# One-bank PSUM items for the S5 half of a kernel that runs a state-space layer beside a long convolution

## The chip, the cores and the metric

The kernel runs on one core of one Trainium2 chip. The metric is the device time of one execution in microseconds (us). The core has four engines that matter here: TensorE (PE, matrix products into PSUM; its weight loads are listed as PEld), VectorE (DVE), ScalarE (ACT) and GpSimd (POOL). SyncE (SP) issues nearly all transfers (DMA). Each engine takes its instructions in the order in which they were written, and waits where an instruction needs a result of another engine.

PSUM holds eight banks; a bank takes 512 fp32 values on each of 128 partitions. In this kernel it is four tiles of two banks each.

## The reference

Two independent parts are computed from their own inputs and laid side by side in the output (2048 positions, 640 columns each, bf16).

```python
# A: a diagonal complex state-space layer (S5), 640 states
dt = exp(log_dt);  Lam_bar = exp(dt * Lam)
B_bar = ((Lam_bar - 1) / Lam)[:, None] * Bmat
Bu = einsum("bld,pd->blp", x, B_bar)
for t in range(L):                      # L = 2048
    h = Lam_bar * h + Bu[:, t, :]
y = 2 * einsum("blp,dp->bld", hseq, Cmat).real + x * Dskip

# B: H3, a 4-tap shift, a gate, a convolution as long as the sequence, a gate
kv = shift(k, shift_k) * v
y = irfft(rfft(pad(kv)) * rfft(pad(ssm_k)))[:S] + kv * ssm_D
return q * y
```

## The kernel before, in words

**Part A.** The 2048 positions are dealt into eight classes c (position modulo 8) of M = 256 positions; the 640 states into five blocks j of 128. In the tile `u{j}` each class has a real and an imaginary plane (r = 0, 1) of 256 columns. For every j the kernel forms, on TensorE, the input products of classes 1 and 5 together (item `u1{j}`), 3 and 7 together (`u3{j}`), 2 and 6 together (`v{j}`), class 4 (`w{j}`) and class 0 (`z{j}`). All of them are products of the transposed weights `BT` with the transposed input `xT` (L460 for pairs of classes, L468 for a single class), five matmuls over the input columns for each plane. `v`, `w` and `z` also gather earlier classes: the function `join` (L475, L476) adds matmuls whose weights are diagonal matrices of powers of the decay (`diagL{j}`, written by item `dL{j}`) and whose data are classes already evicted to `u{j}`. Each product is evicted from PSUM to `u{j}` by an item with an e behind its letter (`ue`, `ve`, `we`, `ze`), by a copy on ScalarE (L144) or VectorE (L146). Then VectorE runs the scan over class 0 (`rs{j}`, `ro{j}`), and the other classes are restored from it: `m{c}{j}` scales by the decay into the tile `tmp` (three instructions, L312 on ScalarE or L314 on VectorE) and `r{c}{j}` adds twice on VectorE (L522).

The outputs are 16 blocks of 128 positions by 640 columns. Item `p{n}` computes one on TensorE: for each half of 320 columns ten matmuls of `u` with `Cs` (L534), and for the first three blocks some small ones for the term x * Dskip (L541). For the other 13 blocks that term is read from the input again (`xl{n}`, a transfer; `xm{n}`, a product at L563), and VectorE adds it while it evicts the block (`ye{n}`, L549). The first three are evicted by ScalarE. `yd{n}` stores a block. Blocks 0 and 1 need class 0 of all j, 2 and 3 class 4, 4 to 7 the classes 2 and 6, 8 to 11 the classes 1 and 5, 12 to 15 the classes 3 and 7. The output staging tile `yo` holds four blocks, and so does the staging of `xl`.

**Part B.** The 640 channels go through in five groups G of 128. A group's stages: `kT`, `vT` (transposing loads), `tap` (the shift, TensorE) and `kv` (VectorE, L625), `kvo` and `kvs` (to memory and back in another order), `hs` (the filter), `s1h`, `s1k` (first transform stage, TensorE L639) with their evictions to the tile As (`s1he`, `s1ke`), `s2` (second stage, L657) with evictions to the tile XH (`s2e`), the spectral product `y` in two halves (VectorE, L671 to L674), `inv` (inverse, L685) with evictions `zs` to the tile zz, `zt` (two transposing transfers of zz), `fin` (last stage, L707), `ob` (product with q on VectorE, L712, for which `qi` loads q) and `od` (store). Each transform item fills a two-bank tile and is evicted by one instruction of 1024 values a partition. `ks` are copies of kT into kS for the shift.

**Order.** A plan (`make_plan`) lists the items with engine, dependences and costs. The order in which they are issued is a written list, `ORDER`, one word for an item. `u10@6` means that item `u1` of block 0 uses the PSUM tile 6 // 2 = 3; a `v` behind it (`ue12@2v`) puts an eviction or a scaling on VectorE, otherwise it runs on ScalarE; `a` and `b` are the two halves of `tmp`. At the end of the kernel a loop walks the list and calls each item's function with its tile. All engines and the queue of SP follow this one list, each with its own items.

The names of the two staging values that the order depends on are `NPS = 4` (PSUM tiles) and `NYO = 4`, `NXR = 4` (output and input staging).

Of the kernel before, what the change touches and what calls it, by code (L numbers as in the profile page):

```python
# [9 lines left out]
ALU = mybir.AluOpType  # L10
# [10 lines left out]
NT = 5  # L21
T = 8
M = L // T
# [4 lines left out]
NYO = 4  # L28
NSK = 13
NXR = 4  # L30
NTAB = 3
# [16 lines left out]
class Kernel:  # L48
# [406 lines left out]
    def pe_u(self, j, c, joins, ps):  # L455
        mm = self.nc.tensor.matmul
        x = self.__dict__[f"xT{c}"]
        for r in range(2):
            for k in range(NT):
                mm(ps[:, r, :], lhsT=self.BT[:, r, k, j * 128:(j + 1) * 128], rhs=x[:, :, k, :],  # L460
                   start=(k == 0), stop=(not joins and k == NT - 1))
        self.join(j, joins, ps, lambda c2, r: self.pair(j, c2, r), 2 * M)

    def pe_w(self, j, c, joins, ps):
        mm = self.nc.tensor.matmul
        for r in range(2):
            for k in range(NT):
                mm(ps[:, r, 0:M], lhsT=self.BT[:, r, k, j * 128:(j + 1) * 128], rhs=self.xc(c)[:, k, :], start=(k == 0), stop=False)  # L468
        self.join(j, joins, ps, lambda c2, r: self.u(j, c2, int(c2 > c))[:, r, :], M)

    def join(self, j, joins, ps, src, n):
        mm = self.nc.tensor.matmul
        for r in range(2):
            for i, (s, c2) in enumerate(joins):
                mm(ps[:, r, 0:n], lhsT=self.dl(j)[:, 3 * s, :], rhs=src(c2, r), start=False, stop=False)  # L475
                mm(ps[:, r, 0:n], lhsT=self.dl(j)[:, 3 * s + 2 - r, :], rhs=src(c2, 1 - r), start=False, stop=(i == len(joins) - 1))  # L476

    def ev_u(self, eng, j, c, ps):
        out = self.__dict__[f"u{j}"][:, c::4, :, 2:2 + M].rearrange("p c r m -> p r c m")
        self.copy(eng, out, ps[:].rearrange("p r (c m) -> p r c m", c=2))  # L480

    def ev_half(self, eng, j, c, ps):
        self.copy(eng, self.u(j, c), ps[:, :, 0:M])
# [20 lines left out]
    def classes(self, j, c):  # L504
        u = self.__dict__[f"u{j}"]
        if c == 4:
            return 1, 6, u[:, 0:1, :, 2:2 + M], u[:, 4:5, :, 2:2 + M]
        if c == 2:
            return 2, 3, u[:, 0::4, :, 2:2 + M], u[:, 2::4, :, 2:2 + M]
        return 2, 0, u[:, c - 1::4, :, 2:2 + M], u[:, c::4, :, 2:2 + M]  # L510
# [13 lines left out]
    def pe_proj(self, c, i, skip, ps):  # L524
        mm = self.nc.tensor.matmul
        ts = slice(128 * i, 128 * i + 128)
        xT = self.xc(c)
        for b in range(2):
            o = ps[:, b, :]
            c0 = 320 * b  # L530
            for j in range(NT):
                h = self.u(j, c)
                for r in range(2):
                    mm(o[:, 0:320], lhsT=h[:, r, ts], rhs=self.Cs[:, r, j, c0:c0 + 320], start=(j == 0 and r == 0),  # L534
                       stop=(skip and j == NT - 1 and r == 1))
            if skip:
                continue
            pieces = [(d, max(c0, d * 128), min(c0 + 320, d * 128 + 128)) for d in range(NT)]
            pieces = [q for q in pieces if q[1] < q[2]]
            for q, (d, lo, hi) in enumerate(pieces):  # L540
                mm(o[:, lo - c0:hi - c0], lhsT=xT[:, d, ts], rhs=self.diagD[:, d, lo - d * 128:hi - d * 128],  # L541
                   start=False, stop=(q == len(pieces) - 1))

    def ev_y(self, eng, n, ps):
        out = self.yo[:, n % NYO, :].rearrange("q (b n) -> q b n", b=2)
        self.copy(eng, out, ps[:, :, 0:320])

    def dve_yx(self, n, ps):
        self.nc.vector.tensor_tensor(out=self.yo[:, n % NYO, :].rearrange("q (b n) -> q b n", b=2), in0=ps[:, :, 0:320],  # L549
                                     in1=self.xr(n).rearrange("q (b n) -> q b n", b=2), op=ALU.add)  # L550
# [168 lines left out]
def make_plan(K):  # L719
# [96 lines left out]
    for c in (1, 5, 3, 7, 2, 6, 4, 0):  # L816
        dmat(f"x{c}", 1.4, 0.3275, (), lambda c=c: K.load_x(c))
    for j in range(NT):
        bt = [f"bte{j}_{x}" for x in range(2)] if j < JB else [f"B{(j - 1) // 2 * 2 + 1}"]
        A(f"dL{j}", "AD", 2.6, ["lam", "dc"] + ([f"z{j - NDL}"] if j >= NDL else []), lambda eng, j=j: K.diagL(eng, j), lat=0.12, dve=1.25)  # L820
        for c in (1, 3):
            pe(f"u{c}{j}", 10 * P512, 20, [f"x{c}", f"x{c + 4}"] + bt + [f"wm{w}" for w in range(WARM)], lambda ps, j=j, c=c: K.pe_u(j, c, (), ps), f"u{c}{j}")
            ev(f"ue{c}{j}", 1024, [f"u{c}{j}", "zer"], lambda eng, ps, j=j, c=c: K.ev_u(eng, j, c, ps), f"u{c}{j}")
        pe(f"v{j}", 14 * P512, 28, ["x2", "x6", f"dL{j}", f"ue1{j}"] + bt, lambda ps, j=j: K.pe_u(j, 2, ((0, 1),), ps), f"v{j}")
        ev(f"ve{j}", 1024, [f"v{j}", "zer"], lambda eng, ps, j=j: K.ev_u(eng, j, 2, ps), f"v{j}")
        pe(f"w{j}", 18 * P256, 36, ["x4", f"dL{j}", f"ue3{j}", f"ve{j}"] + bt, lambda ps, j=j: K.pe_w(j, 4, ((0, 3), (1, 2)), ps), f"w{j}")
        ev(f"we{j}", 512, [f"w{j}", "zer"], lambda eng, ps, j=j: K.ev_half(eng, j, 4, ps), f"w{j}")
        pe(f"z{j}", 22 * P256, 44, ["x0", f"we{j}"] + bt, lambda ps, j=j: K.pe_w(j, 0, ((0, 7), (1, 6), (2, 4)), ps), f"z{j}")
        ev(f"ze{j}", 512, [f"z{j}"], lambda eng, ps, j=j: K.ev_half(eng, j, 0, ps), f"z{j}")
        dve(f"rs{j}", 2.2, [f"ze{j}", f"tab{j}", "lam"], lambda j=j: K.dve_scan(j))  # L830
        dve(f"ro{j}", 1.08, [f"rs{j}"], lambda j=j: K.dve_out(j))
        for c in (4, 2, 1, 3):
            src, raw = {4: ("ro", "we"), 2: ("r4", "ve"), 1: ("r4", "ue1"), 3: ("r2", "ue3")}[c]
            A(f"m{c}{j}", "AD", 1.36 if c == 4 else 2.23, [f"{src}{j}"], lambda eng, buf, j=j, c=c: K.re_mul(eng, j, c, buf), lat=0.12,
              dve=0.73 if c == 4 else 0.9, take=f"R{c}{j}")
            dve(f"r{c}{j}", 0.75 if c == 4 else 1.28, [f"m{c}{j}", f"{raw}{j}", f"z{j}"], lambda buf, j=j, c=c: K.dve_re(j, c, buf), give=f"R{c}{j}")
    zs_all = [f"{x}{j}" for j in range(NT) for x in ("u1", "u3", "v", "w", "z")]
# [3 lines left out]
    for n, (c, i) in enumerate(seq):  # L841
        hs = [f"r{'o4'[c // 4] if c % 4 == 0 else c % 4}{j}" for j in range(NT)]
        skip = n >= 16 - NSK
        pe(f"p{n}", 20 * P320 + 0.3 * (not skip), 40 + 14 * (not skip), hs + cs_all + ["dD"], lambda ps, c=c, i=i, skip=skip: K.pe_proj(c, i, skip, ps), f"p{n}")
        free = f"yd{n - NYO}" if n >= NYO else f"cs{NT - 1}"
        if skip:
            dma(f"xl{n}", "SP", 0.43, 0.107, [f"ye{n - NXR}"] if n >= 16 - NSK + NXR else zs_all, lambda c=c, i=i, n=n: K.load_xr(c, i, n))
            dve(f"xm{n}", 0.4, [f"xl{n}", "dbc"], lambda n=n: K.dve_xm(n))
            dve(f"ye{n}", 0.78, [f"p{n}", f"xm{n}", free], lambda ps, n=n: K.dve_yx(n, ps), give=f"p{n}")
        else:  # L850
            ev(f"ye{n}", 640, [f"p{n}", free], lambda eng, ps, n=n: K.ev_y(eng, n, ps), f"p{n}")
        dma(f"yd{n}", "SP", 0.43, 0.107, [f"ye{n}"], lambda c=c, i=i, n=n: K.store_y(c, i, n))
# [48 lines left out]
zer pc x5 pc2 lv dc B0 wt wm1@0 x1 wm2@2 gp3 dc2 pv@4 exp@4 vec@4 pp2 pc3 zd pp B1 x7 hk rho Fi wm3@6 bt0_1@0 rr bt0_0@2 l_sk aM  # L901
x3 bte0_0@2 bte0_1@0v x6 x2 trig1 lam gam dL0@v dL1@v kT0 G3 hp1 wm0@4 dD u10@6 nG3 u11@0 dcol ue10@6 x4 u12@2 u30@4 ue12@2v hp0
tp0 sk gp1 ks0_1@v vT0 gp2 gp0 G2 ue11@0 v0@6 x0 ue30@4 i64 dS0 tab0 hs0 u31@0 ve0@6 ks0_0@v aR dco dM w0@4 ue31@0v tp2 nG2
tap0_1@2 dR tap0_0@6 B3 we0@4v z0@0 tp1 kv0_1@2 tab1 tp3 kv0_0@6 G1 had0 s1h0_3@4 G0 dS1 H1 dL2@v s1h0_2@2 s1h0_0@6 ze0@0 rs0
ro0 m40@av tab2 v1@0 s1he0_3@4 u13@4 H0 r40@a nI kvo0 kT1 tp4 ve1@0 ks1_0@v tab3 vT1 s1he0_2@2 w1@0 ks1_1@v m20@bv tap1_0@2
r20@b kv1_0@2 nG0 s1he0_0@6 tap1_1@6 kv1_1@6 ue13@4 we1@0 m10@a r10@a s1h0_1@4 s1he0_1@4 z1@0 ze1@0 kvs0 s1k0_3@2 s1k0_2@6 dL3@v
s1ke0_2@6 hs1 s1ke0_3@2 rs1 ro1 u34@4 ue34@4 s1k0_0@0 nG1 s1ke0_0@0 s1k0_1@6 s1ke0_1@6 tab4 v3@2 ve3@2 dS2 had1 s20_2@4 s2e0_2@4
s20_0@0 m30@bv s2e0_0@0v s20_1@6 s2e0_1@6 s20_3@2 s2e0_3@2v kT2 s20_4@4 s20_5@0 s20_6@6 kvo1 s2e0_4@4 s2e0_5@0 m41@av s20_7@2
s2e0_7@2 ks2_1@v s2e0_6@6v u14@4 ue14@4 s1h1_2@0 s1h1_1@2 s1he1_2@0 r41@a s1he1_1@2 CT1 kvs1 vT2 u33@6 s1h1_0@4 ue33@6 s1k1_0@0
ks2_0@v CT0 tap2_0@2 y0_0 tap2_1@6 s1ke1_0@0 s1he1_0@4 s1k1_3@0 s1ke1_3@0 kv2_0@2 kv2_1@6 kT3 s1h1_3@2 y0_1 inv0_0@4 zs0_0@4  # L910
s1k1_1@0 inv0_1@6 zs0_1@6 ca0 s1ke1_1@0v cs0 s1he1_3@2 v2@4 kvo2 ve2@4 inv0_2@6 zs0_2@6 inv0_3@2 s1k1_2@0 dS3 w3@4 s1ke1_2@0
s21_5@6 hs2 ks3_0@v m11@av zs0_3@2 ks3_1@v had2 s21_6@0 we3@4 r11@a s21_4@2 s2e1_4@2v ca1 s2e1_6@0 vT3 zt0_1 u32@4 s2e1_5@6
ue32@4 s21_7@0 s2e1_7@0 kvs2 cs1 ca2 s21_3@2 tap3_0@6 kv3_0@6 tap3_1@4 s2e1_3@2 w2@0 we2@0 s21_2@6 s21_0@2 kv3_1@4 s2e1_2@6
# [22 lines left out]
def kernel(  # L936
# [26 lines left out]
    with tc.manual_schedule():  # L963
        for n, _, how in names:
# [7 lines left out]
            elif tiles:  # L972
                args.append(tiles[0])
# [31 lines left out]
```

## Time and profile before

| | |
|---|---|
| timed runs, median of 3 | 197.34 us (195.78 to 197.46) |
| profiled execution | 197.87 us, its span 195.8 us |
| TensorE busy | 179.1 us, 3135 matmuls |
| VectorE busy | 176.1 us, 365 instructions |
| ScalarE busy | 150.7 us, 199 instructions |
| mean granted TensorE clock | 0.983 |
| 16 DMA engines, the transfers' queue | 89.6% of the span |

A row of the groups reads: line, engine, operation, output and inputs by the program's names, partitions and elements, count; then busy us and the mean ns of one; then idle time of the engine just before, and what ended it. A row of the stretches reads: from and to, length, then busy us of PE, PEld, DVE, ACT and POOL with instruction counts, the granted TensorE clock, the DMA share and GB/s. A row in order of time reads: start, duration, engine, line, operation, count.

### The profile page before, as it was taken

The page shows a single profiled execution, that of the slowest core. Times are in us where ns is not written, and L with a number is a line of the kernel's source. Part 1 is how long each engine was busy: PE and PEld are TensorE (multiplying, and loading weights), DVE is VectorE, ACT ScalarE, POOL GpSimd, SP SyncE. Part 2 cuts the span into 40 slices and gives each one's busy share as a digit, 9 for nine tenths or more (in the row PEclk, how much of TensorE's full clock was granted, in tenths as well). Part 3 has the DMA queues.
Part 4 walks back from the last instruction along what each step waited for, and adds up shares of the span by engine and source line. Part 5 has one row for each costly group of instructions (what it writes and reads, how often), then busy time and mean ns, then how long its engine had stood idle before and what let it go on. Part 6 is the DMA issues. An engine that isn't in the chain of part 4 may idle for free. (4 is left out here: it accounts for less than half of the span.)

```text
span 195.8 us, 7219 instructions
## 1 busy us (share of the span) xinstructions
PE 179.1 (91%) x3135; PEld 123.1 (63%) x3135; DVE 176.1 (90%) x365; ACT 150.7 (77%) x199; POOL 19.7 (10%) x46
## 2 busy tenths in 40 slices
PE   7399999999989999999999866999989999999992
PEld 2144456467474557688667655777677778777771
DVE  1579999999999989999999999999999999998672
ACT  2488478998898999989989899998999794840000
POOL 8874060300000000000000000000000000000000
PEclk9859999999999999999999999999999999999999
DMA  4999799999998999998799994998543994899953
GB/s 91 178 200 164 166 186 176 256 163 166 238 193 175 192 251 200 168 233 203 59 219 152 180 278 85 173 188 200 122 113 83 218 194 90 236 182 245 243 146 118
DMA packets 131966, 34.87 MB, mean 178 GB/s; under 512 B 127200, under 2 KB 131296, under 8 KB 131936
## 3 DMA queue, kind: packets, MB, share of 16 engines
q1 hardware_dynamic: 131608, 34.10, 89.6%
q10 hardware_dynamic: 328, 0.33, 1.3%
q8 instruction: 24, 0.39, 0.8%
q14 instruction: 6, 0.05, 0.1%
HBM read 10.50 MB, written 7.86 MB: 94 GB/s over the span
## 5 line engine op out<-in xcount | busy, mean ns | idle before, releaser
L534 PE MATMUL ps<-Cs,u 128*128 128x320 bf16 x320 | 45.4, 299 | 0.6 <-ACT XH L144 0.5
L534 PEld LDWEIGHTS <-u 128*128 128x128 bf16 x320 | 30.6, 98 | 12.8 <-issue 0.5
L144 ACT CAST As<-ps 128x1024 bf16<-128x1024 f32 x39 | 37.9, 1032 | 0.6 <-PE ps L639 0.5
L144 ACT CAST XH<-ps 128x1024 bf16<-128x1024 f32 x36 | 34.5, 1037 | 2.1 <-PE ps L657 2.1
L460 PE MATMUL ps<-xT,BT 128*128 128x512 bf16 x150 | 35.8, 392 | 0.2 <-ACT zz L144 0.2
L460 PEld LDWEIGHTS <-BT 128*128 128x128 bf16 x150 | 14.5, 100 | 18.3 <-issue 2.6
L522 DVE TENSOR_TENSOR u<-tmp,u 128x1024 bf16<-128x1024 bf16 (+1 forms) x40 | 24.6, 622 | 1.0
L144 ACT CAST u<-ps 128x1024 bf16<-128x1024 f32 (+1 forms) x22 | 18.4, 843 | 8.4 <-PE ps L460 4.7
L144 ACT CAST zz<-ps 128x1024 bf16<-128x1024 f32 x20 | 19.6, 1035 | 2.6 <-DMA zz<-zz 2.5
L657 PE MATMUL ps<-As,Gre 64*64 64x256 bf16 x320 | 19.4, 274 | 2.3 <-DVE vT L625 1.0
L657 PE MATMUL ps<-As,Gim 64*64 64x128 bf16 x320 | 18.1, 216 | 0.0
L657 PE MATMUL ps<-As,nGim 64*64 64x128 bf16 x320 | 18.1, 216 | 0.0
L476 PE MATMUL ps<-u,diagL 128*128 128x256 bf16 (+1 forms) x60 | 15.3, 290 | 0.1
L475 PE MATMUL ps<-u,diagL 128*128 128x256 bf16 (+1 forms) x60 | 15.4, 290 | 0.0
L312 ACT ACTIVATE tmp<-u,lam 128x512 bf16<-128x512 bf16 (+1 forms) x18 | 14.2, 877 | 1.5 <-DVE u L522 1.5
L657 PEld LDWEIGHTS <-Gre 64*64 64x64 bf16 x320 | 11.0, 106 | 5.5 <-issue 4.9
L685 PE MATMUL ps<-XH,I 64*128 64x128 bf16 x320 | 11.6, 216 | 2.2 <-ACT As L144 1.0
L712 DVE TENSOR_TENSOR qb<-ps,qb 128x1024 bf16<-128x1024 f32 x10 | 11.9, 1218 | 1.6 <-DMA qb<-in_B_q_dram 1.6
L549 DVE TENSOR_TENSOR yo<-ps,BT 128x640 bf16<-128x640 f32 x13 | 10.5, 817 | 3.0 <-PE ps L534 3.0
L672 DVE TENSOR_TENSOR XH<-XH 128x2048 bf16<-128x2048 bf16 x10 | 12.2, 1225 | 0.8 <-DVE tmp L671 0.5
L314 DVE TENSOR_SCALAR tmp<-u,lam 128x512 bf16<-128x512 bf16 (+2 forms) x42 | 12.7, 360 | 0.2
L468 PE MATMUL ps<-xT,BT 128*128 128x256 bf16 x100 | 12.6, 273 | 0.0
(166 smaller groups left out, 310.6 us busy)
## 6 DMA issues: line engine op xcount, KB each, us to landing
h_st<-in_B_ssm_k_dram SPq DMA_DIRECT2D x10, 256.0 KB, 4.4
kv_rows<-vT SPq DMA_DIRECT2D x5, 512.0 KB
kv_st<-kv_rows SPq DMA_DIRECT2D x10, 256.0 KB, 4.2
qb<-in_B_q_dram SPq DMA_DIRECT2D x10, 256.0 KB, 4.2
out_dram<-qb SPq DMA_DIRECT2D x10, 256.0 KB, 4.7
out_dram<-yo SPq DMA_DIRECT2D x16, 160.0 KB, 3.2
BT<-in_A_x_dram SPq DMA_DIRECT2D x13, 160.0 KB, 3.2
zz<-in_A_B_re_dram ACTq DMA_DIRECT2D x1, 160.0 KB, 5.1
```

Of the source, the lines that this page charges most:

```text
L144: self.nc.scalar.copy(out=out, in_=in_)
L312: self.nc.scalar.activation(out=out, in_=in_, func=ACT.Copy, scale=w)
L314: self.nc.vector.tensor_scalar_mul(out=out, in0=in_, scalar1=w)
L460: mm(ps[:, r, :], lhsT=self.BT[:, r, k, j * 128:(j + 1) * 128], rhs=x[:, :, k, :], start=(k == 0), stop=(not joins and k == NT - 1))
L468: mm(ps[:, r, 0:M], lhsT=self.BT[:, r, k, j * 128:(j + 1) * 128], rhs=self.xc(c)[:, k, :], start=(k == 0), stop=False)
L475: mm(ps[:, r, 0:n], lhsT=self.dl(j)[:, 3 * s, :], rhs=src(c2, r), start=False, stop=False)
L476: mm(ps[:, r, 0:n], lhsT=self.dl(j)[:, 3 * s + 2 - r, :], rhs=src(c2, 1 - r), start=False, stop=(i == len(joins) - 1))
L522: v.tensor_tensor(out=o, in0=buf[:, i, 0:n], in1=o, op=ALU.add)
L534: mm(o[:, 0:320], lhsT=h[:, r, ts], rhs=self.Cs[:, r, j, c0:c0 + 320], start=(j == 0 and r == 0), stop=(skip and j == NT - 1 and r == 1))
L657: mm(out, lhsT=w[rows, k, :], rhs=rhs, start=(w is self.Gre), stop=(w is self.Gim))
L672: tt(out=X, in0=X, in1=pl(0, 1).to_broadcast([128, 8, 2, 128]), op=ALU.mult)
L712: self.nc.vector.tensor_tensor(out=q, in0=ps[:].rearrange("p b (m e) -> p b m e", e=32), in1=q, op=ALU.mult)
```

## The change

The S5 products become items of one PSUM bank.

- `u1`, `u3` and `v` of a block j are split by plane r: `u10_0` and `u10_1` in place of `u10`, each with its own eviction of 512 values (`u10e_0`, `u10e_1`). The joins of a `v` half follow its five input products directly; before, the joins of both planes came after all ten.
- `w` and `z` stay one item each, but put their two planes of 256 columns side by side in one bank, where they had used the lower half of two.
- The output blocks `p{n}` are split into their two column halves, `p{n}_0` and `p{n}_1`, each evicted by its own instruction of 320 values. The store `yd{n}` waits for both, and so does the reload of the input staging.
- The digit behind `@` is now a bank for these items: `u10_1@1` is the second bank of tile 0. Transform items keep whole tiles.
- A branch for other forms of `v` (`JV`) is added and is empty.
- `ORDER` is new: 646 words for 584. Which evictions and scalings run on VectorE is chosen anew with it.

| ScalarE / VectorE | before | after |
|---|---|---|
| evictions of `u1`, `u3`, `v`, 1024 values | 13 / 2 | none |
| the same, 512 values | none | 23 / 7 |
| evictions of `w` and `z`, 512 values | 9 / 1 | 10 / 0 |
| evictions to As | 39 / 1 | 38 / 2 |
| evictions to XH | 36 / 4 | 40 / 0 |
| outputs with and without the x term | 3 of 640 / 13 of 640 | 6 of 320 / 26 of 320 |
| scalings `m4` | 0 / 5 | 2 / 3 |
| scalings `m1`, `m2`, `m3` | 6 / 9 | 5 / 10 |
| copies to kS | 0 / 10 | 2 / 8 |
| evictions to BT: 1024, 256 values | ScalarE, VectorE | VectorE, ScalarE |

The diff, cut to its core:

```diff
-    def pe_u(self, j, c, joins, ps):
+    def pe_u(self, j, c, r, joins, ps):
+        x = self.__dict__[f"xT{c}"]
+        for k in range(NT):
+            self.nc.tensor.matmul(ps, lhsT=self.BT[:, r, k, j * 128:(j + 1) * 128], rhs=x[:, :, k, :],
+                                  start=(k == 0), stop=(not joins and k == NT - 1))
+        self.join(j, r, joins, ps, lambda c2, r: self.pair(j, c2, r))
+
+    def pe_w(self, j, c, joins, ps):
+        for r in range(2):
+            o = ps[:, M * r:M * r + M]
...
+    def ev_u(self, eng, j, c, r, ps):
+        self.copy(eng, self.__dict__[f"u{j}"][:, c::4, r, 2:2 + M], ps.rearrange("p (c m) -> p c m", c=2))
...
-    def pe_proj(self, c, i, skip, ps):
+    def pe_proj(self, c, i, b, skip, ps):
...
+    def ev_y(self, eng, n, b, ps):
+        self.copy(eng, self.yo[:, n % NYO, 320 * b:320 * b + 320], ps[:, 0:320])
+
+    def dve_yx(self, n, b, ps):
+        s = slice(320 * b, 320 * b + 320)
+        self.nc.vector.tensor_tensor(out=self.yo[:, n % NYO, s], in0=ps[:, 0:320], in1=self.xr(n)[:, s], op=ALU.add)
...
+    def pair(nm, j, c, deps, joins):
+        n = 5 + 2 * len(joins)
+        for r in range(2):
+            pe(f"{nm}_{r}", n * P512, 2 * n, deps, lambda ps, r=r: K.pe_u(j, c, r, joins, ps), f"H{nm}_{r}")
+            ev(f"{nm}e_{r}", 512, [f"{nm}_{r}", "zer"], lambda eng, ps, r=r: K.ev_u(eng, j, c, r, ps), f"H{nm}_{r}")
...
+                key = (it["take"] or [it["give"] or it["use"]])[0]
+                tile_ = K.ps[int(slot) // 2]
+                args.append(tile_[:, int(slot) % 2, :] if key[0] == "H" else tile_)
```

Of the new order, TensorE's items from the last spectral ones on (before, then after):

```
s24_2 p7 p6 p4 inv4_0 inv4_2 inv4_1 inv4_3 fin3_1 fin3_0 p10 p9 p8 fin4_0 fin4_1 p11 p14 p13 p12 p15

s24_3 p4_1 p11_0 fin3_1 fin3_0 inv4_2 p9_1 p9_0 inv4_0 p8_0 inv4_3 inv4_1
p10_1 p8_1 p10_0 p11_1 p14_0 p13_1 p14_1 p15_0 fin4_0 fin4_1 p15_1 p12_1 p12_0 p13_0
```

SP's queue around the moved transfers (before, then after):

```
kT2 kvo1 CT1 kvs1 vT2 CT0 kT3 kvo2 ... zt2_1 kvs4 zt2_0 yd0 od1 ... od2 yd2 yd3 qi3 zt3_0 xl4 zt3_1 ... yd7 zt4_0 yd5 zt4_1

kT2 kvo1 hs1 vT2 CT0 kvs1 kT3 kvo2 CT1 ... xl6 yd1 xl3 dbc kvs4 od1 ... od2 zt3_1 zt3_0 yd7 qi3 ... yd9 xl13 zt4_1 xl8 zt4_0
```

185 lines of the change are left out of this document (89 added, 96 removed).

## The prediction

> **What bounds the kernel now.** I read the shares of the span first, then stretches of time, then the chain of waits, and last each engine's list of instructions in order of time.
>
> ```profile
> span 195.8 us, 7219 instructions
> PE 179.1 (91%) x3135; PEld 123.1 (63%) x3135; DVE 176.1 (90%) x365; ACT 150.7 (77%) x199; POOL 19.7 (10%) x46
> ```
>
> Two engines are near nine tenths, so the share alone names no bound. The table by stretches does (after each stretch: its length, then the busy time of each engine):
>
> ```profile
> 0.00:12.00 12.00, 7.44 (x28) 3.05 (x29) 4.55 (x28) 5.10 (x12) 9.53 (x33) 0.85 0.85 148
> 12.00:50.00 38.00, 38.00 (x301) 20.86 (x301) 36.36 (x116) 31.73 (x57) 10.15 (x14) 0.96 1.03 182
> 50.00:105.00 55.00, 53.29 (x1120) 36.73 (x1118) 53.40 (x89) 52.06 (x63) 0.00 (x0) 1.00 1.02 194
> 105.00:125.00 20.00, 15.24 (x483) 12.61 (x472) 19.54 (x28) 18.68 (x22) 0.00 (x0) 1.00 0.89 167
> 125.00:178.00 53.00, 50.96 (x1104) 39.76 (x1106) 51.79 (x91) 43.17 (x50) 0.00 (x0) 1.00 0.85 169
> 178.00:195.80 17.80, 14.21 (x134) 10.11 (x126) 10.40 (x16) 0.00 (x0) 0.00 (x0) 1.00 0.63 179
> 35.00:165.00 130.00, 121.88 (x2527) 87.95 (x2526) 126.60 (x221) 120.17 (x145) 1.70 (x2) 1.00 0.93 177
> ```
>
> From 12 to 50 TensorE never stops. From 50 to 178 VectorE is the full one, and ScalarE is close behind it up to 157. After 178 ScalarE has nothing left and TensorE runs projections alone. In the wide stretch of the last row TensorE idles 8.1 us, ScalarE 9.8, VectorE 3.4: what a new order can win lies there and in the last stretch. The chain ends so:
>
> ```profile
> 171.77 5.51 DMA zz<-zz
> ...
> 177.32 1.20 PE ps L707 x64
> 178.52 13.70 PE ps L534 x100
> 192.22 0.02 issue
> 192.25 0.82 DVE yo L549
> ```
>
> The last transform group's transposed blocks land at 177.28; its two final products and then five whole projection blocks (100 matmuls, 0.137 us each) follow on TensorE. What stands ahead of that on the engines:
>
> ```profile
> 128.78 4.68 ACT L144 CAST XH<-ps 128x1024 bf16<-128x1024 f32 x5
> 157.27 4.65 ACT L312 ACTIVATE tmp<-u,lam 128x1024 bf16<-128x1024 bf16 x6
> 164.37 3.76 ACT L144 CAST zz<-ps 128x1024 bf16<-128x1024 f32 x4 [2.45 <-DMA zz<-zz]
> 161.97 0.68 DVE L674 TENSOR_TENSOR XH<-XH,tmp 128x1024 bf16<-128x1024 bf16 x1
> 163.37 1.96 PE L685 MATMUL ps<-XH,I 64*128 64x128 bf16 x64
> ```
>
> So the spectral product `y4_0` ends on VectorE at 162.65, the inverse products `inv4` on TensorE at 165.33, their evictions `zs4` on ScalarE at 168.13. From there to the landing are 9.15 us.
>
> **The change, part by part.** No matmul is added or taken away: TensorE's work stays, and its end moves only by idle time won or lost. The sum is therefore made at one point, the last `inv4`, from which the new order's rest is fixed.
>
> *TensorE behind that point.* The new order puts behind the last `inv4` eight half projections, the two final products `fin4`, and four more halves. A half is 10 matmuls, 1.37 us by the chain's row; the two `fin4` are 2.4. So TensorE ends 12 x 1.37 + 2.4 = 18.8 us after the last `inv4`, where it is now 26.9 (165.33 to 192.22). In return, four halves and two `fin3` have moved ahead of it: 4 x 1.37 + 2.4 = 7.9 us. With none of its idle time saved, the last `inv4` ends at 173.2.
>
> *VectorE ahead of it.* Prices, from instructions that run back to back (a group's mean overlaps the next by about 0.09):
>
> ```profile
> 162.98 1.54 DVE L549 TENSOR_TENSOR yo<-ps,BT 128x640 bf16<-128x640 f32 x2
> 107.36 2.35 DVE L625 TENSOR_TENSOR vT<-ps,vT 128x1024 bf16<-128x1024 f32 x2
> 142.98 2.81 DVE L522 TENSOR_TENSOR u<-tmp,u 128x1024 bf16<-128x1024 bf16 x4
> 168.30 1.00 DVE L314 TENSOR_SCALAR tmp<-u,lam 128x1024 bf16<-128x1024 bf16 x3
> 127.81 0.74 DVE L314 TENSOR_SCALAR tmp<-u,lam 128x512 bf16<-128x512 bf16 x3
> L549 DVE TENSOR_TENSOR yo<-ps,BT 128x640 bf16<-128x640 f32 x13 | 10.5, 817 | 3.0 <-PE ps L534 3.0
> L625 DVE TENSOR_TENSOR vT<-ps,vT 128x1024 bf16<-128x1024 f32 x10 | 11.8, 1217 | 0.3 <-PE ps L620 0.3
> L563 DVE TENSOR_TENSOR BT<-BT 128x640 bf16<-128x640 bf16 x13 | 6.0, 483 | 0.0
> L146 DVE COPY kS<-kT 64x1032 bf16<-64x1032 bf16 x10 | 4.7, 470 | 0.2
> ```
>
> An output of 640 takes 1.54 - 0.82 = 0.72, one of 1024 takes 2.35 - 1.22 = 1.13: 1.07 ns an element, so (estimates by that line) 0.38 for 320 and 0.59 for 512. Ahead of the end of `y4_0` the new order has, against the old: four more additions of L522 for class 1 (+2.8); two more three-part scalings at 1.00 and two fewer of the small kind at 0.74 (+0.5); seven 512 evictions where there were five more 1024 ones and one 512 (-2.1); the 1024 part of BT instead of its 256 part (+0.8); two copies of kS fewer (-0.9); ten half output additions for three whole (+1.6); one product of L563 more (+0.4). Sum +3.1 us: at the old idle time `y4_0` ends at 165.8. Over the whole run VectorE gets 2.2 us lighter (13 output additions split at 2 x 0.38 - 0.72 = +0.5; evictions -2.1; scalings -0.5; kS -0.9; BT +0.8); that is off the path while TensorE ends last.
>
> The Trainium skill, "Perfetto Trace Analysis", section Optimizing Scalar/DVE Operations, speaks against the splits: an instruction pays about 125 ns on VectorE for touching PSUM and 51 on ScalarE, and a full engine gains by larger ones. By that the 13 splits on VectorE would cost 1.6 us instead of 0.5; the rows decide here.
>
> *ScalarE ahead of the last `zs4`.*
>
> ```profile
> 41.74 1.51 ACT L144 CAST u<-ps 128x1024 bf16<-128x1024 f32 x2
> L144 ACT CAST u<-ps 128x1024 bf16<-128x1024 f32 x13 | 13.1, 1010 | 6.3 <-PE ps L460 4.7 <-PE ps L476 1.6
> L144 ACT CAST u<-ps 128x512 bf16<-128x512 f32 x9 | 5.4, 600 | 2.1 <-PE ps L476 2.1
> L144 ACT CAST yo<-ps 128x640 bf16<-128x640 f32 x3 | 2.1, 698 | 0.7 <-PE ps L541 0.7
> L312 ACT ACTIVATE tmp<-u,lam 128x512 bf16<-128x512 bf16 x12 | 8.0, 730 | 0.0
> L312 ACT ACTIVATE tmp<-u,lam 128x1024 bf16<-128x1024 bf16 x6 | 7.0, 1171 | 1.5 <-DVE u L522 1.5
> ```
>
> The first row is a 1024 and a 512 eviction together, 1.51 less the second's 0.60: 0.92 and then 0.51 in a row. Thirteen evictions at 0.92 become 23 halves at 0.51, with one more of `w` (+0.3). Four more of XH and one fewer of As at 4.68/5 = 0.94 (+2.8). Six half outputs for three whole ones, 0.35 each by 0.8 ns an element from 0.61 (+0.3). Two small scalings at about 1.5 (+3.0; 0.64 and twice 0.42, the line through 730 and 1171 less the overlap). Two copies of kS, for which ScalarE has no row; between the 1024 eviction's 0.94 and 1.17 I take 1.1, its lines being about as long (+2.2). The small part of BT for the large (-0.6). Sum +7.9 us. With none of ScalarE's idle time saved the last `zs4` ends at 168.1 + 7.9 = 176.0.
>
> *How much idle time is recovered.* This is the open term.
>
> ```profile
> ACT u L144 <- PE ps L476: 2.0, 3, 0.9
> ACT u L144 <- PE ps L460: 1.3, 2, 1.0
> ```
>
> Both rows are of the stretch 35 to 105: 3.3 us in which ScalarE stood before a whole S5 block that TensorE was still writing. With one-bank items the first half can go while the second is written, and eight products instead of four can stand in PSUM. Another 2.5 us is the wait for the transposed blocks of the group before (row at 164.37); the new order puts those two transfers directly behind one another on SP's queue, ahead of a store and a load of q. I take recovery between 3.3 and 5.8, at 4.6. The bounds are nothing (0) and all 9.8; the latter is cut off by VectorE: `y4_0` at 165.8, then on TensorE three `inv4` (0.49 each) and one half projection, 168.7.
>
> *The sum.* Last `zs4` 176.0 - 4.6 = 171.4, last `inv4` 1.0 before it, 170.4. TensorE would have to save 173.2 - 170.4 = 2.8 of its 8.1 us of idle. TensorE's end 170.4 + 18.8 = 189.2. The transfer does not overtake it: 171.4 + 9.15 = 180.6, while TensorE comes to `fin4` at 170.4 + 8 x 1.37 = 181.4. Then the last half addition, 0.48 (817 less 320 elements at 1.04), and what now follows the last VectorE instruction, 195.8 - 193.07 = 2.73. Span 192.4.
>
> *What I cost at nothing.* The reordering at the start (BT's large part on VectorE, the real scale later on ScalarE, `gam` behind `dL0`): TensorE is full from 12 to 50 and eight half products of over 1 us precede the first that needs `dL0`; without that cover it costs about 1 us. The moved transfers on SP (`CT1` behind `kvo2`, `kvs4` behind `yd1`, `zt4_1` behind `yd9`): behind a store that waits for a half output stand the next loads, but `CT1` has some 12 us of VectorE work between it and its user, and `yd9` comes before `zs4` ends; a slip shows one for one in `fin4`. The waits for both halves of a class ask no more than the whole item did. The branch for `JV` is empty and issues nothing.
>
> **The rivals.**
>
> *Nothing recovered.* ScalarE works 52.06 of the 55 us from 50 to 105 already, and the added 7.9 us may simply push `y3` and `y4`. Last `zs4` 176.0, `inv4` 175.0, TensorE 193.8, span 197.0. For it: seven half projections stand ahead of the fourth group's last spectral item on TensorE, where one whole block stood. Against it: the long S5 waits lie exactly in the items that are halved.
>
> *Slower: ScalarE's waits grow with its items.*
>
> ```profile
> ACT u L144 <- PE ps L460: 4.7, 4, 2.8
> ACT u L144 <- PE ps L476: 3.8, 5, 1.1
> ```
>
> That is 8.5 us over 22 evictions of `u`, 0.39 each. An in-order ScalarE that meets 33 of them and waits as long at each loses 4.3 us more: last `zs4` 180.3, `inv4` 179.3, TensorE 198.1, span 201.3. Place: the evictions of `u` between 35 and 105 and what is queued behind them, XH above all, for which VectorE waits at `y`. It decides once the last `zs4` ends after about 177.
>
> *The clock.*
>
> ```profile
> 115.00:120.00 5.00, 3.40 (x120) 2.81 (x120) 4.90 (x8) 4.54 (x5) 0.00 (x0) 1.00 0.60 183
> ```
>
> TensorE idled 1.6 of 5 us here and kept its full clock, so short pauses between bank-sized groups should not lower it. Were the 150 products of 512 columns run at half clock even for a third of their 35.8 us, it would cost 12 us: span 204. The Trainium skill, "TensorE: Matmul & The Clock Gate", section A second HAM failure mode, describes such a drop where 512-column groups cycle through banks; the row above bears it out nowhere.
>
> *The halves are not independent.* If the order between engines is kept by whole two-bank tiles, a half waits for its neighbour's eviction, up to 0.60 at each of 72 half products. A quarter of them exposed is 11 us: span about 203. No row shows two engines on the two banks of one tile.
>
> **How the numbers follow.** The profiled execution took 197.87 us for a span of 195.8, 2.07 around it; the median of the timed runs is 197.34, 0.53 below. So span 192.4 is 194.0 us as a median. All recovered: `inv4` 168.7, span 190.7, 192.3 us. Nothing recovered: 198.6. Waits growing: 202.9.
>
> Chances: my forecast, recovery of 3 us or more, 0.50; little or nothing recovered 0.29; growing waits 0.14; clock 0.04; coupled halves 0.03. One per cent, about what a measurement tells apart here (the runs before lie 0.85% apart), is 195.4 and 199.3 us. The first case lies below it, the second between, the last three above: 0.50, 0.29, 0.21. The range goes from a little under the fully recovered case to the unrecovered one: 191 to 199, which leaves out the slower cases.
>
> **What would show it.** ScalarE's waits for L460 and L476 before `u` down from 8.5 us while their count rises, and no 2.5 us before `zs4`: then recovery is right. ScalarE's busy time near 156 (7.9 more, less one set of three scalings, 4.65/2, that goes to VectorE at the end), VectorE's near 174: the price list is right. The last `zz` eviction near 171 and only some 40 projection matmuls behind the last L707: the tail is right. It is wrong if VectorE shows new waits before L671 (spectral products late), if the clock falls below 1.00 after 20 us, or if the last `zz` eviction comes after 176.

## The result: 11% slower, most of it waiting

| | before | after |
|---|---|---|
| timed runs, median | 197.28 us of 4 (195.78 to 197.46) | 218.99 us of 4 (218.60 to 222.37) |
| after over before, 95% interval | | 1.111 (1.104 to 1.118) |

The profiled execution of the kernel after took 222.37 us with a span of 220.4, 3.4 us above the median; it is 1.7% above the fastest of the four, so its trace is read for where the time went, and the ratios, which leave such an execution out, for how much. Its page begins:

```profile
span 220.4 us, 7239 instructions
PE 182.5 (83%) x3135; PEld 122.3 (55%) x3135; DVE 176.2 (80%) x374; ACT 156.4 (71%) x221; POOL 19.1 (9%) x46
PEclk9995699996979999999999999999999999999999
```

The busy times are those of the forecast (ScalarE 156.4, where 156 was expected; VectorE 176.2 for 174). The engines do the work that was priced, and 24.6 us of span have come on top. The stretches show where (length, then busy time of PE, PEld, DVE, ACT, POOL, then the granted clock):

```profile
12.00:50.00 38.00, 24.03 (x163) 12.15 (x162) 26.84 (x87) 21.55 (x43) 8.67 (x12) 0.86 0.75 146
50.00:90.00 40.00, 31.95 (x431) 18.96 (x431) 28.88 (x57) 27.17 (x40) 0.00 (x0) 0.92 0.78 149
90.00:130.00 40.00, 38.32 (x775) 27.20 (x776) 36.43 (x60) 37.74 (x49) 0.00 (x0) 1.00 0.80 150
130.00:178.00 48.00, 43.80 (x1086) 33.94 (x1078) 44.62 (x80) 43.88 (x53) 0.00 (x0) 1.00 0.78 170
178.00:220.40 42.40, 35.47 (x668) 26.39 (x660) 33.50 (x58) 18.46 (x21) 0.00 (x0) 1.00 0.72 172
```

From 12 to 50 TensorE, which had been full there, works 24.0 of 38 us, and no other engine is full in its place; up to 90 us it is much the same. Most of the S5 products stand in these 80 us. The table of waits (engine and line that waited, for whom: us in all, times, longest):

```profile
ACT u L145 <- PE ps L459: 19.5, 5, 10.5
PE ps L459 <- DVE u L147: 9.7, 1, 9.7
ACT u L145 <- PE ps L474: 9.0, 4, 3.8
DVE yo L546 <- PE ps L531: 7.0, 7, 1.9
PE ps L459 <- ACT u L145: 6.3, 6, 1.6
PE ps L531 <- DVE yo L546: 3.0, 4, 1.2
```

TensorE waits for evictions and the evicting engines wait for TensorE. Two later profiles of the same kernel, with spans of 220.4 and 219.9 us, show the same waits, some of other lengths: 15.1 and 15.2 us for the first row, 4.2 and 4.0 us for the second. The largest single wait of TensorE, in order of time:

```profile
9.31 3.41 PE L459 MATMUL ps<-xT,BT 128*128 128x512 bf16 x15 [0.46 <-DVE BT L147]
22.39 8.38 PE L459 MATMUL ps<-xT,BT 128*128 128x512 bf16 x30 [9.66 <-DVE u L147]
```

and what VectorE did at its end:

```profile
15.13 2.75 DVE L315 TENSOR_SCALAR diagL<-ident,lam 128x128 bf16<-128x128 bf16 x9
...
21.57 0.17 DVE L345 TENSOR_SCALAR gam<-gam 128x10 f32<-128x10 f32 x1
21.65 0.68 DVE L147 CAST u<-ps 128x512 bf16<-128x512 f32 x1
```

After 15 matmuls, that is after the halves `u10_0`, `u10_1` and `u12_0`, TensorE stands for 9.66 us until VectorE has evicted `u12_0`. The next product in its order is `u11_0`, which goes to bank 3. It needs neither the data of `u12_0` nor its bank, which is bank 2. But banks 2 and 3 are one tile, and the program's waits are made by the tile: `u11_0` writes a tile from which an eviction written ahead of it has still to read. That eviction, `u12e_0@2v`, stands in VectorE's queue behind `lam`, `dL0`, `nG0` and `gam`.

### The profile page after: what moved, and what is told of

Its sections match the earlier page's. It is cut to its first block, busy times and chain, and to the rows that moved or that the text cites. A ratio compares the mean times of both kernels' runs of the same rounds, so it can differ in the third digit from the quotient of the medians.

```text
span 220.4 us, 7239 instructions
## 1 busy us (share of the span) xinstructions
PE 182.5 (83%) x3135; PEld 122.3 (55%) x3135; DVE 176.2 (80%) x374; ACT 156.4 (71%) x221; POOL 19.1 (9%) x46
## 5 line engine op out<-in xcount | busy, mean ns | idle before, releaser
L459 PE MATMUL ps<-xT,BT 128*128 128x512 bf16 x150 | 38.7, 401 | 17.5 <-DVE u L147 9.7
L145 ACT CAST XH<-ps 128x1024 bf16<-128x1024 f32 x40 | 38.5, 1037 | 2.7 <-PE ps L653 2.5
L145 ACT CAST u<-ps 128x512 bf16<-128x512 f32 x33 | 18.8, 597 | 29.6 <-PE ps L459 19.5
L145 ACT CAST As<-ps 128x1024 bf16<-128x1024 f32 x38 | 37.7, 1028 | 1.9 <-PE ps L635 1.7
L459 PEld LDWEIGHTS <-BT 128*128 128x128 bf16 x150 | 14.5, 102 | 37.4 <-issue 23.1
L521 DVE TENSOR_TENSOR u<-tmp,u 128x1024 bf16<-128x1024 bf16 (+1 forms) x40 | 24.6, 624 | 3.8 <-ACT tmp L313 2.9
L145 ACT CAST zz<-ps 128x1024 bf16<-128x1024 f32 x20 | 19.9, 1024 | 3.9 <-PE ps L681 2.6
L467 PE MATMUL ps<-xT,BT 128*128 128x256 bf16 x100 | 15.3, 286 | 4.0 <-ACT u L145 3.4
L546 DVE TENSOR_TENSOR yo<-ps,BT 128x320 bf16<-128x320 f32 x26 | 12.2, 487 | 7.5 <-PE ps L531 7.0
L473 PE MATMUL ps<-u,diagL 128*128 128x256 bf16 (+1 forms) x60 | 16.7, 302 | 0.0
L474 PE MATMUL ps<-u,diagL 128*128 128x256 bf16 (+1 forms) x60 | 16.6, 301 | 0.0
L621 DVE TENSOR_TENSOR vT<-ps,vT 128x1024 bf16<-128x1024 f32 x10 | 12.0, 1216 | 5.5 <-issue 2.9
L653 PEld LDWEIGHTS <-Gre 64*64 64x64 bf16 x320 | 10.6, 106 | 8.8 <-issue 8.4
L313 ACT ACTIVATE tmp<-u,lam 128x512 bf16<-128x512 bf16 (+2 forms) x21 | 15.0, 784 | 0.6 <-DVE u L488 0.6
L467 PEld LDWEIGHTS <-BT 128*128 128x128 bf16 x100 | 9.6, 101 | 7.2 <-issue 5.1
L703 PE MATMUL ps<-Mq,zz 128*64 128x64 bf16 x640 | 11.9, 196 | 0.9 <-issue 0.5
```

Of the source, the lines that this page charges most:

```text
L145: self.nc.scalar.copy(out=out, in_=in_)
L313: self.nc.scalar.activation(out=out, in_=in_, func=ACT.Copy, scale=w)
L459: self.nc.tensor.matmul(ps, lhsT=self.BT[:, r, k, j * 128:(j + 1) * 128], rhs=x[:, :, k, :], start=(k == 0), stop=(not joins and k == NT - 1))
L467: self.nc.tensor.matmul(o, lhsT=self.BT[:, r, k, j * 128:(j + 1) * 128], rhs=self.xc(c)[:, k, :], start=(k == 0), stop=False)
L473: mm(o, lhsT=self.dl(j)[:, 3 * s, :], rhs=src(c2, r), start=False, stop=False)
L474: mm(o, lhsT=self.dl(j)[:, 3 * s + 2 - r, :], rhs=src(c2, 1 - r), start=False, stop=(i == len(joins) - 1))
```

## The experiments

Theory 1: all items of a two-bank tile are held in the written order, whichever bank they touch; the halves are not independent. Theory 2: the new order itself is at fault, with VectorE's long queue ahead of the first halves, and a TensorE clock that falls in the pauses. Theory 3: the greater number of items is.

| run | order | waits | ratio to before (95% interval) |
|---|---|---|---|
| after, and twice more | new | by the tile | 1.111 (1.104 to 1.118), 1.111 (1.102 to 1.120), 1.115 (1.101 to 1.128) |
| banks free | new | by the bank | 0.974 (0.970 to 0.978) |
| halves cut in place | old | by the tile | 0.996 (0.990 to 1.001) |
| the same, banks free | old | by the bank | 0.997 (0.994 to 1.000) |
| one swap | new, one item moved | by the tile | 1.073 (1.069 to 1.077) |
| S5 products free, outputs held | new | both kinds | 1.002 (0.998 to 1.006) |
| outputs free, S5 products held | new | both kinds | 1.081 (1.074 to 1.089) |
| products free, evictions held | new | both kinds | 1.023 (1.014 to 1.032) |
| eight tiles of one bank | new | by the bank | 0.979 (0.972 to 0.985) |
| pause filled, 36 matmuls | new | by the tile | 1.118 (1.112 to 1.124) |
| pause filled, 16 matmuls | new | by the tile | 1.100 (1.085 to 1.114) |

### The same order with waits by the bank

Nothing is moved. For two items of one tile that touch different banks, and of which the later does not need the earlier's data, the wait is left out; each bank gets its own waits. Core of the edit:

```diff
+        for name0, banks0, ins0 in old:
+            if banks0 & banks or name0 in deps:
+                continue
+            for a in ins:
+                for b in (i for i in ins0 if i.engine != a.engine):
+                    self.tc.declare_no_dep(a, b, reason="other bank")
+        for b in banks:
+            k = (tile_, b)
+            if is_pe:
+                for e in self.r.get(k, []):
+                    self.tc.add_manual_dep(ins[0], e.name, ..., reason="bank free")
...
+                    self.tc.add_manual_dep(a, self.w[k].name, ..., reason="bank full")
```

> The kernel after, with its order of work, its banks and its instructions unchanged; only the waits between a product into one bank and an eviction out of the other bank of the same tile are left out, and each bank has waits of its own (full before it is evicted, evicted before it is written again). Theory 1 (the halves are held together by the tile: the program orders every access of a two-bank tile, whichever bank it touches): TensorE's 9.66 us before the 15 half products at 22.39 go, ScalarE's idle time in front of L145 falls from 29.6 us to under 10, the granted clock stays above 0.98, and the time comes to 191 to 199 us. Theory 2 (the new order itself, with VectorE's queue in front of the first halves, and a clock that falls in the pause): the waits move to other instructions, and the time stays at 208 us or more. Between 200 and 207 both have a share.

Measured: 193.06 us beside 198.85, ratio 0.974 (0.970 to 0.978). Theory 1 holds. Theory 2 expected 208 us or more; the order and the items are the same in both kernels, and only the waits differ. Its page and the group of S5 half evictions (busy and mean ns, then idle time ahead of them):

```profile
span 190.6 us, 7261 instructions
...
PE 176.5 (93%) x3135; PEld 120.1 (63%) x3135; DVE 174.3 (91%) x374; ACT 156.0 (82%) x221; POOL 19.5 (10%) x46
...
L145 ACT CAST u<-ps 128x512 bf16<-128x512 f32 x33 | 18.5, 593 | 4.5 <-PE ps L474 4.5
```

The same row in the kernel after, where the same 33 evictions had 29.6 us of idle time:

```profile
L145 ACT CAST u<-ps 128x512 bf16<-128x512 f32 x33 | 18.8, 597 | 29.6 <-PE ps L459 19.5
```

And the start on TensorE in order of time, with free banks:

```profile
10.12 9.87 PE L459 MATMUL ps<-xT,BT 128*128 128x512 bf16 x45 [0.50 <-issue]
...
22.29 1.25 PE L459 MATMUL ps<-xT,BT 128*128 128x512 bf16 x5 [1.87 <-DVE u L147]
```

Forty-five matmuls go through in one row where fifteen did. `u12_0` is still evicted late here (21.56 to 22.24 on VectorE), but the wait for it is the true one: the next product after the pause of 1.87 us is the first that uses its bank again.

### The old order with halves cut in place

Each S5 product, join and output block of the old list becomes two words, side by side; the code is that of the kernel after.

```diff
-dD u10@6 nG3 u11@0 dcol ue10@6 x4 u12@2
+dD u10_0@6 u10_1@7 nG3 u11_0@0 u11_1@1 dcol u10e_0@6 u10e_1@7 x4 u12_0@2 u12_1@3
```

> The kernel before with its old order; every S5 product, joined block and output block is cut in halves on the spot: both halves of a product stand next to each other in TensorE's order, both evictions next to each other on the engine that had the whole one. The tiles are as in the kernel after, with the waits that come with them. Theory 1: no other item stands between two halves of one tile, so the waits by the tile bind as they did for the whole pair, and what is left is the price of the 45 added eviction instructions, about 0.4 us on VectorE and up to 3 on ScalarE: 196 to 200 us. Theory 3 (the number of items is the loss: twice as many evictions, each with its waits and its start): 45 more items cost what they cost in the kernel after, 206 us or more.

> As the run with the halves cut in place, and in addition with waits by the bank and not by the tile. Theory 1: the first half is evicted while the second is written (a half product takes 1.1 us, an eviction 0.6), so each pair is free some 0.5 us earlier; ScalarE's waits in front of L145 fall by 1 to 3 us; 194 to 198 us, 0 to 2 us below the run with waits by the tile. Theory 2 has the old order here and expects the same.

Measured: 0.996 with waits by the tile and 0.997 with waits by the bank; both intervals contain 1.000. So neither the number of items nor the coupling costs as much as 1% in the old order. In that list a tile holds the halves of one S5 or output item at a time, from the first product to the last eviction; in the new list more than twenty such items share a tile with another. This takes theory 3 out. It also shows that halves alone win nothing: I had expected ScalarE's waits ahead of L145 to fall by 1 to 3 us with free banks, and they went from 6.3 to 5.7 us (rows: held, then free).

```profile
L145 ACT CAST u<-ps 128x512 bf16<-128x512 f32 x35 | 19.3, 596 | 6.3 <-PE ps L459 3.3 <-PE ps L474 3.0
```

```profile
L145 ACT CAST u<-ps 128x512 bf16<-128x512 f32 x35 | 19.9, 600 | 5.7 <-PE ps L474 4.5 <-PE ps L459 1.2
```

The gain of 2.6% needs the new order together with free banks, and the loss of 11.1% comes from the new order with held ones.

### One item moved

```diff
-u12_0@2 u12e_0@2v x7 u11_0@3
+u12_0@2 u11_0@3 u12e_0@2v x7
```

> The kernel after with its waits by the tile, and with one item moved: the half product u11_0 (bank 3) stands ahead of the eviction u12e_0 (bank 2 of the same tile, on VectorE behind lam, dL0, nG0 and gam) in the written order; TensorE's own order and VectorE's own order stay. Theory 1: the 9.66 us in front of u11_0 go, u12e_0 now waits for the product instead, which is done long before VectorE comes to it; the other couplings stay: 208 to 212 us. Theory 2: the products behind run into VectorE's late evictions all the same, TensorE still pauses 6 us or more in 14 to 30 us, and the time stays at 215 or more.

Measured: 214.96 us beside 198.85, ratio 1.073 (1.069 to 1.077). The pause is gone: L459 waits for VectorE's casts no more, and its largest waits are now for ScalarE.

```profile
PE ps L459 <- ACT u L145: 7.0, 7, 1.6
PE ps L531 <- DVE yo L546: 4.0, 5, 1.4
```

The time in us missed my 208 to 212, which I had reckoned from the first result; this run's before is slower, and by the ratio the first result's 197.28 us would become 211.7. The swap returns 3.8% of before's time, 7.5 us. That is less than the 9.66 of the profiled pause and more than the 4.2 and 4.0 us of the two later profiles: what counts is when the products get through. The first join behind them starts at 22.93 us here, and at 30.61, 28.60 and 28.66 us in the three profiles of the kernel after. Theory 2's pause of 6 us or more behind it is not there. Its figure of 215 us lies next to the median, but is not evidence for it: the couplings that remain hold the time there, as the run with free banks shows. Moving one word gave back a third of the loss against before.

### Which items carry the loss

In the condition of the first run, pairs with an output block are held, or only they are free:

```diff
-            if banks0 & banks or name0 in deps:
+            if banks0 & banks or name0 in deps or not (not any(x.startswith(("p", "ye")) for x in (name, name0))):
```

> The kernel after with waits by the bank for the S5 products and joined blocks (u, v, w, z), and still by the tile wherever an output block (p) or its addition is one of the two. By theory 1 the loss of the kernel after (11.1% of before) and the gain of the run with all banks free (2.6%) differ by 13.7%, some 27 us, and this run divides them: in the trace of after the waits that belong to output blocks are 3.0 us of TensorE for L546, 7.0 of VectorE for L531 and 3.8 of additions that wait for the reloaded x rows, so they should carry the smaller part: 2 to 9 us above the run with all banks free, 195 to 202 us. If the outputs carry most, over 207.

> The counterpart: waits by the bank wherever an output block (p) or its addition is one of the two, by the tile among the S5 products and joined blocks. Theory 1 with the larger part in the products: the pause of 9.7 us at 22 us stays and the clock falls behind it, 205 to 216 us. If the two parts add up, this run's distance from the run with all banks free and that of its counterpart make 27 us together; if the late products also push the outputs into worse places, they make less.

Measured: 199.32 and 215.03 us beside 199.09. Against the run with all banks free, holding the outputs costs 1.002 - 0.974 = 2.8%, holding the S5 products 1.081 - 0.974 = 10.8%, together 13.6%; holding both costs 1.111 - 0.974 = 13.7%. The two parts add up. With only the outputs held, their waits stand in the trace as they do in the kernel after:

```profile
DVE yo L546 <- PE ps L531: 7.1, 7, 2.0
...
PE ps L531 <- DVE yo L546: 3.9, 4, 1.4
```

With only the S5 products held, theirs do:

```profile
ACT u L145 <- PE ps L459: 14.7, 6, 4.9
...
PE ps L459 <- ACT u L145: 6.3, 6, 1.5
```

### Which direction carries it

```diff
-            if banks0 & banks or name0 in deps:
+            if banks0 & banks or name0 in deps or not (is_pe):
```

> The kernel after in which a product no longer waits for an eviction out of the neighbour bank, while an eviction still waits for a product that is written into the neighbour bank ahead of it in the program's order. Theory 1a (what costs is TensorE held by an engine's queue: the eviction stands behind other work there): nearly all is back, 193 to 199 us. Theory 1b (what costs is ScalarE and VectorE held by a later product, with all that stands behind the eviction on those engines): ScalarE's idle time in front of L145 stays over 15 us and the time at 205 or more.

Measured: 204.21 us beside 199.09, ratio 1.023 (1.014 to 1.032), between the two expectations. Freeing the products from a neighbour's eviction gives back 1.111 - 1.023 = 8.8% of the 13.7; the other 4.9% are left to evictions held by a neighbour's product. Both shares have an uncertainty of about one per cent, and the counterpart, with the evictions alone freed, was not run. How that second kind works shows on ScalarE in this run,

```profile
59.11 0.58 ACT L145 CAST u<-ps 128x512 bf16<-128x512 f32 x1 [2.99 <-PE ps L459]
```

and on VectorE:

```profile
59.73 0.42 DVE L486 TENSOR_TENSOR tmp<-tab,u 128x512 bf16<-128x512 bf16 x1 [3.27 <-ACT u L145]
```

`z1` is in bank 4; `u14_1`, in bank 5, stands between `z1` and its eviction in the list. The eviction of `z1` waits for an L459 product that has nothing to do with `z1`, and VectorE's scan of that block waits for the eviction. Not all of the 2.99 us is a false wait: the last matmul of `z1` ends at 57.33 us and the last of `u14_1` at 59.07, so the neighbour's part is 1.7 us.

### Eight tiles of one bank

The same freedom without any exception written in: every bank is a tile, and what was evicted in pairs takes two instructions.

```diff
-        self.ps = [psum.tile([128, 2, 512], f32, name=f"ps{i}") for i in range(NPS)]
+        self.ps = [Pair([psum.tile([128, 512], f32, name=f"ps{i}_{b}") for b in range(2)]) for i in range(NPS)]
...
-        self.copy(eng, out, ps[:].rearrange("p r (k n) -> p r k n", n=8))
+        for r in range(2):
+            self.copy(eng, out[:, r], ps[:, r, :].rearrange("p (k n) -> p k n", n=8))
```

> The kernel after with the eight banks declared as eight tiles of one bank, so that every wait goes by the bank without any exception written in; what was evicted in pairs (transforms, taps, transposed B, last products) is evicted by two instructions of one bank each, in the same place. Theory 1: the 9.7 us pause goes as in the run with free banks. The price: 98 ScalarE evictions of 1024 columns at 1.03 us become 196 at 0.59, 15 us more for ScalarE (156 to 171), and 23 operations of 1.22 on VectorE become 46 at about 0.69, 3.5 us more (174 to 178). ScalarE has 10 us of idle time left in its stretch, so 3 to 12 us above the run with free banks: 196 to 205 us. Theory 2 (order and clock) expects over 210.

Measured: 194.71 us beside 199.09, ratio 0.979 (0.972 to 0.985); its interval overlaps that of the run with exceptions. The page:

```profile
PE 179.2 (93%) x3135; PEld 122.5 (63%) x3135; DVE 174.1 (90%) x397; ACT 160.7 (83%) x320; POOL 19.5 (10%) x46
```

My price was too high. ScalarE has 99 instructions more than with free pairs and is busy 160.7 - 156.0 = 4.7 us longer, 0.05 each, not the 15 us that I had worked out from the group's mean of 593 ns, which includes an overlap with the next instruction. On VectorE the total does not show the 23 more instructions (174.1 for 174.3), but totals of the kernel after alone lie between 172.7 and 176.2. The rows of the products that were cut in two show them (free banks, then one-bank tiles):

```profile
L708 DVE TENSOR_TENSOR qb<-ps,qb 128x1024 bf16<-128x1024 f32 x10 | 12.2, 1221 | 1.1 <-PE ps L703 1.1
L724 DVE TENSOR_TENSOR qb<-ps,qb 128x512 bf16<-128x512 f32 x20 | 12.8, 684 | 1.4 <-ACT yo L154 0.7
```

Ten more instructions take 0.6 us more, 0.06 each, and so do the ten of the product `kv`. With the three of the evictions to As and BT it is 1.5 us for all 23, where I had expected 3.5.

### The pause filled with work

Is it the wait that costs, or the clock that falls in it? From 15 to 25 us the kernel after had (5 us each, the clock is the third number from the end):

```profile
15.00:20.00 5.00, 0.00 (x0) 0.00 (x0) 4.97 (x16) 4.15 (x10) 3.74 (x5) 0.57 1.12 196
20.00:25.00 5.00, 2.62 (x7) 0.96 (x7) 3.25 (x18) 0.00 (x0) 0.79 (x2) 0.50 0.94 180
```

Here matmuls on the identity, whose results nobody reads, stand in the pause, first 36 and then 16; the kernel after runs beside each.

```diff
-x7 u11_0@3
+x7 fill@6 u11_0@3
```

> The kernel after with its waits by the tile, and with 36 matmuls on the identity (as in the warm-up, into tile 3, whose result nobody reads) put into TensorE's order ahead of u11_0: TensorE works through most of its 9.7 us pause and its clock has no reason to fall there; the product that waits for u12e_0 still waits. It divides the wait from the clock. Theory 1 (the waits cost, the clock only follows): the granted clock is near 1.00 from 15 to 30 us, the 30 half products behind the pause take 6.5 us where they took 8.4, and the time falls by no more than 1.9 and at most some 3 us: 215 to 221 us, ratio 1.09 to 1.12. Theory 2 (the clock carries a good part of the 21.7 us): TensorE's busy time without the filling falls from 182.5 to under 178 and the time to 212 or less, ratio under 1.08.

> The kernel after unchanged, beside the run with its pause filled, on the same chip: 217 to 222 us, ratio 1.10 to 1.12.

Measured: 221.40 us, and 220.88 for the kernel after, beside 198.06; ratios 1.118 (1.112 to 1.124) and 1.111 (1.102 to 1.120). The products behind the pause take 6.64 us where they took 8.38, but the filling is too long:

```profile
16.11 7.93 PE L421 MATMUL ps<-ident 128*128 128x512 bf16 x36
23.88 6.64 PE L459 MATMUL ps<-xT,BT 128*128 128x512 bf16 x30
```

VectorE had evicted `u12_0` at 20.36, so the filling itself held the products back some 3.5 us. This run settled nothing, and I took the short one:

> As the run with the pause filled, with 16 matmuls in place of 36: the 36 ended some 3.5 us after u12e_0 (at 20.36 on VectorE) and so held the products back themselves. 16 take 3.5 us and end before it. Theory 1: the clock stays up, the products behind the pause take 6.5 us and end up to 1.7 us earlier than in the kernel after, and the time is 0 to 2 us below it, ratio 1.10 to 1.115. Theory 2: ratio under 1.08.

> The kernel after unchanged, on the same chip: ratio 1.10 to 1.12. The length of the pause differs between executions (9.7 us and 4.2 us in two profiles) with the start of TensorE; its end, set by VectorE, differs less (22.3 and 20.4 us).

Measured: 218.40 us, and 221.30 for the kernel after, beside 199.23; ratios 1.100 (1.085 to 1.114) and 1.115 (1.101 to 1.128). The short filling, in order of time and by stretch:

```profile
15.04 3.62 PE L421 MATMUL ps<-ident 128*128 128x512 bf16 x16
19.75 6.63 PE L459 MATMUL ps<-xT,BT 128*128 128x512 bf16 x30 [1.10 <-DVE u L147]
```

```profile
20.00:25.00 5.00, 5.00 (x25) 2.29 (x24) 3.49 (x6) 1.68 (x3) 3.29 (x5) 1.00 0.82 137
```

The kernel after, in the profile taken beside it:

```profile
20.50 8.32 PE L459 MATMUL ps<-xT,BT 128*128 128x512 bf16 x30 [3.95 <-DVE u L147]
```

```profile
20.00:25.00 5.00, 4.50 (x14) 1.70 (x14) 1.82 (x5) 3.03 (x7) 3.47 (x5) 0.66 0.82 163
```

With the clock held the 30 products take 8.32 - 6.63 = 1.7 us less, and the medians differ by 2.9 us, with intervals that overlap. So the low clock may be worth these 2 to 3 us of the 22 at this place, and theory 2's under 1.08 is not reached; nor does TensorE's busy time without the filling, 187.0 - 3.62 = 183.4 us, fall under 178. Over the whole run the clock's share has a bound. TensorE was busy 182.5, 186.5 and 187.1 us in three profiles with held banks and 176.5 with free ones. A lower clock costs time by lengthening busy time, so its share is at most 6 to 10.6 us, by the profile. TensorE's idle time grew by more, from 14.1 us of the span with free banks to between 32.8 and 37.9 with held ones; so the greater part is waiting. The pause differs between executions, 9.66, 4.2 and 3.95 us in three profiles of the kernel after, by when TensorE starts; its end (22.39, 20.44 and 20.50 us) lies within 2 us, because VectorE's queue sets it.

## Why the prediction was wrong

I predicted 194.0 us, in a range of 191 to 199; the kernel took 218.99.

**The step that failed** is the premise of the open term: "With one-bank items the first half can go while the second is written, and eight products instead of four can stand in PSUM." In this program two halves of a tile follow one another in the written order, product or eviction. Eight products can stand in PSUM only as far as the list has their neighbours evicted ahead of them. With the premise made true, the sum comes out. This is the tail with free banks, ScalarE's last evictions to zz,

```profile
168.23 1.93 ACT L145 CAST zz<-ps 128x1024 bf16<-128x1024 f32 x2 [1.01 <-PE ps L681]
```

and the chain to the end:

```profile
167.64 1.00 PE ps L681 x32
168.64 10.97 PE ps L531 x80
179.61 2.15 PE ps L703 x128
181.75 5.55 PE ps L531 x40
187.31 0.02 issue
187.33 0.49 DVE yo L546
```

The last `inv4` ends at 168.64 (predicted 170.4, with 168.7 for all recovered), the last `zs4` at 170.16 (171.4), and TensorE 187.31 - 168.64 = 18.67 behind `inv4` (18.8). ScalarE's waits for L459 and L474 ahead of `u` are 4.5 us for 8.5. By the sum's own terms 176.0 - 170.16 = 5.8 us are recovered, the top of my 3.3 to 5.8, where I put 4.6. The ratio is 0.974, where 194.0 of 197.34 us is 0.983; in us it is 193.06, beside a slower before. I forecast the kernel that the diff describes and not the one that the program's waits made.

**What I costed at nothing: the start.** I wrote that "eight half products of over 1 us precede the first that needs `dL0`" and that missing cover would cost about 1 us. I asked who needs `dL0` and `gam`. I did not ask what is queued behind them on VectorE, which is `u12e_0`, nor who could be made to wait for that. Held by the tile it was `u11_0`, for 9.66 us in the first profile and 4.2 and 4.0 in the later ones. With free banks TensorE still waits 1.87 us for the same eviction, but at a later product, which needs the bank.

**The rival "the halves are not independent"** named the mechanism and had a chance of 0.03 and a time of 203. The chance was too low: "No row shows two engines on the two banks of one tile" was as much a reason against my own premise, on which 0.50 rested, as against the rival. The price was of the wrong kind. I charged up to 0.60 us, one eviction's duration, for a quarter of the halves. What a held product waits for is the eviction's turn on its engine, with all that stands ahead of it, and the run with one swap shows that one such place gave back 7.5 us. The other direction, evictions held by products, was not in the price at all, and what is left to it above is 4.9% of before's time, near 10 us.

**The rival "ScalarE's waits grow with its items"** would seem borne out by 29.6 us of idle time ahead of 33 evictions. It is not: the same 33 have 4.5 us with free banks. Their number was not the reason.

**The clock** fell (to 0.50 at 20 to 25 us), but not by the groups that cycle through banks, as its rival had it: with free banks the same groups ran at a mean of 1.00. It was low behind the pauses that the waits made, where it may have taken 2 to 3 us at the first of them, and at most 6 to 10.6 in all. One later profile has 0.66 already from 10 to 15 us, ahead of the pause, so not every low stretch comes from the waits.

**The price list** held: ScalarE 156.4 for 156; VectorE 176.2 in this profile and 174.3 with free banks for 174. For ScalarE's pairs cut in two I had charged 2 x 0.51 - 0.92 = 0.10 us; the run with one-bank tiles shows 0.05. The Trainium skill, "Perfetto Trace Analysis", section Optimizing Scalar/DVE Operations, has 51 ns for a ScalarE instruction on PSUM, and this trace agrees. By its 125 ns for VectorE, the 23 instructions added there would be 2.9 us; the rows show 1.5, 0.06 each, so the measurement decides for the smaller price.

## What to carry to other kernels

Before two engines are to work on two parts of one buffer, find out at which grain the program keeps order; a slice of a tile may be a place of its own for the hardware and not for the waits. Where it is the tile, make the tile as small as the item: eight one-bank tiles cost 0.05 us for each pair that ScalarE then evicts in two, and turned 11% of loss into 2% of gain. A false wait costs what is queued ahead of the instruction that it waits for, and so a list of work that gained 2.6% with free parts lost 11.1% when they were held.

## What the runs showed of the hardware

Work of TensorE and of the evicting engines on the two banks of a former pair showed no disturbance here: with free banks the S5 half evictions on ScalarE took 593 ns in the mean, for 597 in the kernel after, and the L459 matmuls 379 ns in the median in both. Behind a pause of 4 us the granted clock was 0.66 from 20 to 25 us, in two profiles, and 30 matmuls took 8.32 us; with the pause filled it was 1.00 and they took 6.63. Sixteen matmuls of no use in that pause made the kernel no slower, and by the medians 1.3% faster, with intervals that overlap.
